# Key exponentials under the activations' second half, w_phi by four loads, layer norm by tiles, and a new order of all steps

## Chip, core and metric

The kernel runs on one core of one Trainium2 chip. The time is device microseconds (us) of one execution, the median of several runs. Engines: TensorE (PE, matmuls; its weight loads are listed as PEld), VectorE (DVE), ScalarE (ACT), GpSimd (POOL) and SyncE (SP, which here only issues DMAs). ACT can issue DMAs too.

## What is computed

One input x (2048 tokens of 448) goes through a layer norm without weights; two branches read the result, and both are added to x.

```python
xn = _layernorm(x)                                   # over 448, eps 1e-5
# A: linear attention, H = 16 heads of Dh = 28
q, k, v = xn @ wqkv
pq, pk = q @ w_phi, k @ w_phi                        # per head, 28 x 28
phi = concat(softmax(p), softmax(-p))                # for q and for k
kv, z = phi_k^T v, sum(phi_k)
o = (phi_q kv) / (phi_q z + 1e-6)
A = o @ wo
# B: feed forward, F = 1792
h = xn @ w1 + b1
B = (h * tanh(softplus(h))) @ w2                     # mish
out = x + A + B
```

The inputs and the output are bfloat16.

## The kernel before, in words

**Units.** The 2048 tokens are 16 tiles t of 128, or 8 units u of two tiles (2u, 2u+1). A unit's normalised pair `xn` is 896 columns; transposed, it is seven blocks of 128 rows, the middle one shared: rows 0 to 63 belong to one tile and rows 64 to 127 to the other. So the matmuls over xn use half the rows of PE at a time (64 rows), two halves side by side into two PSUM banks. `passes` (L418) splits such a block into three parts: A and B (six matmuls each) and H (two, the shared block). A block takes a pair of banks (`pair_part`, L436, `take2`, L390) with its first part and frees it when the last part's reader on ACT or DVE has been recorded. There are four pairs.

**Steps.** `ORDER` (L147) is a hand-kept list of step names; each step appends its instructions to the queues of its engines (`run_order`, L166), so the list is the program order of every engine at once. `Program.resolve` (L89) puts in the semaphore waits. An engine runs its own instructions strictly in that order, the DMAs that SP or ACT issue among them. The names:

- `lx..`, `lkm`, `lkt`, `lvm`, `lqT`, `lp`, `lb`, `l1m`, `l1t`, `l2`, `lo`: loads of x, W_k (main rows and the tails of W_k and W_v), W_v, W_q transposed, w_phi, b1, W1, W2, Wo; the last letter is the issuing queue (s for SP, a for ACT).
- `pi`, `pm`, `pw`, `pv`, `pk`, `pp`, `zero`: constants that POOL sets up. `z12` is twelve matmuls on zeros (`warm`, L369).
- `st`, `rs`, `xn`: layer norm of a unit: mean and variance (`ln_stats`, L459; DVE's bn instructions, or with b the odd tile on ACT), 1/sqrt (`ln_rstd`, L477; a on ACT, p on POOL), and the scaled pair (`ln_pair`, L491; d on DVE, p on POOL). `xt`: the pair's transpose (`xT`, L524), by PE with copies on ACT or DVE, or by a DMA of SP (m).
- `wtk`, `wmk`, `wmq`, `bd`: q and k are never formed: W_q and W_k are multiplied by w_phi first (`w_tr` L555, `w_mm` L578), w_phi lying block-diagonally in `Wbd`, which `w_bd` (L547) fills from `Wraw` and a mask.
- `v`, `k`, `q` with unit and part: the products of xn with W_v and the two folded weights. `k` and `q` end with two exponentials on ACT (plus and minus), into `E_of(u)` (L230) and `Eq_of(u)` (L235).
- `kn`u.s: one half's sums over the 28 features on DVE, their reciprocals, and the product on POOL (`k_norm`, L633). `kv`: 16 matmuls a unit, all units into one pair of banks; `kvz`: DVE takes it out, a DMA transposes it.
- `e`t: a DMA transpose of a tile's query exponentials (L695). `nd`t: 16 short matmuls for numerators and denominators, then seven DVE instructions (L723). `ot`u: transpose of the attention's result. `wo`: its product with Wo.
- `f`q.c: one block of 128 of the 1792 hidden features for half q of the tokens (q = 0 or 1, 1024 tokens), then one mish on ACT into `actT` (`ffn1`, L706). `g`t: 14 full-row matmuls with W2 for a tile (`ffn2`, L831). The last of a tile's `wo` and `g` adds x on DVE (`finish`, L798), and `sto`, `stt` store.

**Shared memory.** `actT` holds for each of 14 feature blocks a row of 2048 tokens. The key exponentials of unit u lie in row 6 + u of it, columns 0 to 1791, so they cover a part of both halves; query exponentials use rows 4 and 5 and a buffer of their own in turn. A mish over such a row waits for all that read it.

**Rows.** Blocks in parts and `nd` use half-row matmuls; the transposes, the weight products, `kv` and `g` use more than 64 rows. PE changes from one row mode to the other 14 times after the warm-up.

Of the kernel before, what the change touches and what calls it, by code (L numbers as in the profile page):

```python
# [170 lines left out]
def _kernel(es, nc, A_x, A_wqkv, A_w_phi, A_wo, B_w1, B_b1, B_w2, out):  # L171
# [284 lines left out]

    def ln_stats(u, both=False):  # L459
# [527 lines left out]
```

## Time and profile before

| | us |
|---|---|
| time, median of 3 runs | 155.51 (154.67, 155.51, 155.71) |
| span of the profiled execution, first to last instruction | 153.4 |
| busy: PE, PEld, DVE, ACT, POOL | 145.5, 74.4, 105.3, 73.3, 40.1 |

The page gives the span of the profiled execution and no run time for it. Times in rows are microseconds from the start of this span. A timeline row is: start, length, engine, source line, operation, what is written and read, count, and in brackets the idle time before it and what ended it; neighbouring instructions of a kind are merged. A row of a window is its bounds, its length, and the busy time of PE, PEld, DVE, ACT and POOL with their counts, the granted clock of PE, the busy share of the DMA engines and what they moved. A row of DMA issues gives count, size and the median time from issue to landing.

### The profile page before, as it was taken

Reading aid. Unit: us, or ns where it says so; the run is one execution under the profiler, and the core shown is the slowest. Engines: PE = TensorE matmul, PEld = TensorE weight load, DVE = VectorE, ACT = ScalarE, POOL = GpSimd, SP = SyncE. Lnnn points to the kernel's source line nnn. Section 1 sums busy time; section 2 is a strip of 40 time slices with the busy share of each in tenths; the row PEclk is TensorE's granted clock in tenths of the full one; section 3 lists DMA queues with packets and bytes.
Section 4 is the critical chain, followed back from the end, with each engine's and each line's share of the span. In section 5 each row is a group of like instructions: output and inputs, shape, how many; then the busy total and the mean of one; then the engine's idle time right before and its main releaser. Section 6 shows DMA issues by size and latency. Waiting matters only on the chain.

```text
span 153.4 us, 3609 instructions
## 1 busy us (share of the span) xinstructions
PE 145.5 (95%) x1541; PEld 74.4 (48%) x1541; DVE 105.3 (69%) x229; ACT 73.3 (48%) x89; POOL 40.1 (26%) x58
## 2 busy tenths in 40 slices
PE   6898998999899999999988999999999999999993
PEld 2364553554344475445434446554555555545552
DVE  1699999999999903078767399995699600693521
ACT  4974998684899896967674673000500000000000
POOL 5562384465999991000000000000000000000000
PEclk9999999999999999999999999999999999999999
DMA  4996656797989309898990303303020320005331
GB/s 128 251 272 198 145 88 133 184 300 148 131 140 195 77 0 85 172 268 164 338 139 14 60 4 64 60 0 60 27 99 0 75 44 4 0 0 129 122 113 60
DMA packets 39964, 17.22 MB, mean 112 GB/s; under 512 B 33932, under 2 KB 39180, under 8 KB 39948
## 3 DMA queue, kind: packets, MB, share of 16 engines
q1 hardware_dynamic: 39776, 16.89, 52.0%
q8 instruction: 12, 0.20, 0.5%
q10 hardware_dynamic: 172, 0.10, 0.2%
q14 instruction: 4, 0.03, 0.1%
...
## 4 chain that ended last, share of the span: by engine, by line
PE 71%; DVE 17%; DMA 6%; POOL 2%; issue 1%; ACT 1%; DVEq 0%; POOLq 0%
PE PS L433 29%; PE PS L836 28%; PE PS L853 7%; DVE xn L507 5%; DMA Wkv<-xn 4%; PE PS L374 3%; DVE stats L472 3%; PE PS L657 2%; PE PS L731 2%; DMA xnT<-xn 2%; DVE Sk L636 2%; DVE v_all L522 2%; POOL xn L502 1%; ACT actT L689 1%; DVE mv L474 1%
## 5 line engine op out<-in xcount | busy, mean ns | idle before, releaser
L433 PE MATMUL PS<-xnT,W 64*128 64x512 bf16 x392 | 45.3, 376 | 0.4 <-DVE v_all L752 0.4
L708 ACT ACTIVATE actT<-PS,b1T 128x1024 bf16<-128x1024 f32 x28 | 30.2, 1113 | 27.2 <-PE PS L433 27.2
L836 PE MATMUL PS<-W,actT 128*128 128x448 bf16 (+1 forms) x224 | 42.7, 351 | 0.0
L836 PEld LDWEIGHTS PS<-W,actT 128*128 128x128 bf16 x224 | 21.6, 98 | 20.2 <-issue 0.7
L433 PEld LDWEIGHTS PS<-xnT,W 64*128 64x128 bf16 x392 | 17.8, 94 | 22.5 <-PE PS L433 2.4
L640 POOL TENSOR_TENSOR actT<-actT,rSk 128x896 bf16<-128x896 bf16 x16 | 26.7, 1699 | 4.8 <-DVE rSk L638 4.8
L801 DVE TENSOR_TENSOR x_all<-PS,x_all 128x448 bf16<-128x448 f32 (+1 forms) x16 | 9.4, 616 | 18.9 <-PE PS L836 15.5
L636 DVE TENSOR_REDUCE Sk<-actT 128x32 f32<-128x896 bf16 x16 | 16.7, 1046 | 0.0
L433 PE MATMUL PS<-Wpk,xnT 64*128 64x448 bf16 x112 | 13.8, 349 | 1.1 <-DMA xnT<-xn 0.7
L628 ACT ACTIVATE actT<-PS 128x896 bf16<-128x896 f32 x16 | 13.7, 927 | 2.4 <-PE PS L433 2.4
L433 PE MATMUL PS<-Wkv,xnT 64*128 64x448 bf16 x112 | 13.6, 349 | 0.0
L433 PE MATMUL PS<-Wpq,xnT 64*128 64x448 bf16 x112 | 12.7, 349 | 0.4 <-ACT actT L689 0.4
L746 DVE COPY Sq<-PS 128x16 f32<-128x16 f32 x32 | 4.0, 167 | 12.5 <-PE PS L731 12.5
L757 DVE TENSOR_TENSOR xn<-v_all,rden 128x448 bf16<-128x448 f32 x16 | 10.0, 625 | 2.4 <-DMA Wkv<-xn 1.9
L472 DVE BATCH_NORM_STATS2 stats<-x_all 128x6 f32<-128x448 bf16 x14 | 8.4, 601 | 3.4 <-DMA x_all<-in_A_x_dram 3.4
L754 DVE TENSOR_TENSOR v_all<-v_all 128x464 f32<-128x464 f32 x16 | 10.3, 642 | 0.6
L750 DVE TENSOR_TENSOR v_all<-PS,Sq 128x464 f32<-128x464 f32 x16 | 10.3, 641 | 0.5
L752 DVE TENSOR_TENSOR v_all<-PS,Sq 128x464 f32<-128x464 f32 x16 | 10.1, 630 | 0.0
L689 ACT ACTIVATE actT<-PS 128x896 bf16<-128x896 f32 x10 | 8.6, 917 | 3.0 <-PE PS L433 2.9
L507 DVE TENSOR_SCALAR xn<-x_all,mv,rstd 128x448 bf16<-128x448 bf16 (+2 forms) x21 | 9.5, 507 | 0.1
L433 PEld LDWEIGHTS PS<-Wpk,xnT 64*128 64x128 bf16 x112 | 5.3, 94 | 6.7 <-DVE v_all L522 1.6
L433 PEld LDWEIGHTS PS<-Wpq,xnT 64*128 64x128 bf16 x112 | 5.4, 94 | 6.1 <-ACT actT L689 0.8
...
## 6 DMA issues: line engine op xcount, KB each, us to landing
...
out_dram<-x_all SPq DMA_DIRECT2D x7, 224.0 KB, 2.1
...
x_all<-in_A_x_dram SPq DMA_DIRECT2D x4, 224.0 KB, 3.2
...
W<-in_B_w_dram SPq DMA_DIRECT2D x2, 224.0 KB, 3.6
```

What stands on the lines that cost most here:

```text
L433: ins = e.matmul(o, lhs(c, k), rhs(c, k), start=first and n == at[par][0], stop=last and n == at[par][-1])
L472: op("DVE", lambda e, t=t: e.bn_stats(stats[:, t, :], x_all[:, t, :]), r=[("x", t)], w=[("st", t)], tag=f"bn{t}")
L507: op("DVE", lambda e, t=t, lo=lo, hi=hi, at=at: e.tensor_scalar(X[:, at:at + hi - lo], x_all[:, t, lo:hi], mv[:, t, 0:1], rstd[:, t:t + 1] ...
L628: op("ACT", lambda e, s=s: e.activation(E_of(u)[:, s, :, :], two(b, D), ACT.Exp, scale=1.0 if s == 0 else -1.0), r=[pb(b), pb(b + 1)], w=[ ...
L636: op("DVE", lambda e: e.tensor_reduce(Sk[u][:, s, :], Eh(), AX.X, ALU.add), r=[("E", u, s)], w=[("Sk", u, s)], tag=f"Sk{u}.{s}")
L640: op("POOL", lambda e: e.tensor_tensor(Eh(), Eh(), ap_on(rSk[u][:, s, 0:1], [[1, 2 * H], [0, DH]]), ALU.mult), r=[("E", u, s), ("rSk", u, ...
L689: op("ACT", lambda e, s=s: e.activation(Eq_of(u)[:, :, s, :].rearrange("p i (h n) -> p i h n", n=64)[:, :, :, 0:QP], two(b, D).rearrange(" ...
L708: op("ACT", lambda e: e.activation(actT[:, fc, q * 1024:(q + 1) * 1024], bank(b, 2), ACT.Mish, bias=b1T[:, fc:fc + 1]), r=[("b1T",), pb(b) ...
L750: op("DVE", lambda e: e.tensor_tensor(tv(t1[i]), num(0), sx(1), ALU.mult), r=[pb(b), pb(b + 1), ("Sq", i, 1)], w=[("t1", i)], tag=f"ta{t}")
L754: op("DVE", lambda e: e.tensor_tensor(t1[i], t1[i], t2, ALU.add), r=[("t1", i), ("t2",)], w=[("t1", i)], tag=f"tc{t}")
L836: ins = e.matmul(bank(b)[:, 0:width(t)], actT[:, fc, tok(t)], W2[:, fc, 0:width(t)], start=first and fc == 0, stop=last and fc == FC - 1)
L853: ins = e.matmul(bank(b)[:, 0:w], oT_of(u)[lo:hi, cc * P:(cc + 1) * P], Wo[lo:hi, cc, 0:w], start=first and n == at[par][0], stop=last and ...
```

## The change

- **Where exponentials lie.** `actT` is laid out by halves of the tokens. All eight key blocks lie in the second half (q = 1) one after another; query exponentials of units 1, 4, 7 and 2, 5 lie in the first half's rows 10, 11 and 12, 13. A mish of the second half now waits for the key blocks under it (`E_under`), one of the first half for none of them.
- **w_phi.** Four small DMAs put its blocks straight into `Wbd`, after `pw` has cleared it. `Wraw`, the mask (`pm`) and the two products on POOL (`bd`) go.
- **Layer norm by tiles.** `st`t, `xn`t (and `rt`t for the root of one tile, `rs`u for two) are steps of one tile each, on DVE (d), ACT (a) or POOL (p). In the new order ACT takes the statistics of tile 5 and scales tile 0; POOL scales tiles 4, 5, 8, 11, 12 and 13; DVE does the rest. Before, ACT took the statistics of tiles 5 and 7, POOL scaled tiles 10 and 11.
- **Loads of x** by any run of tiles. The first part of the loads is divided: ACT issues tiles 1, 4 and 5, 2 and 3, w_phi, W_v, 6 and 7, later 12 to 15, and Wo; SP tiles 0, W_k, the tails, 8 and 9, b1, W_q transposed, later 10 and 11.
- **`kc`u** (`k_norm2`): sums and reciprocals of both halves of a key block in one instruction each; used for units 2 and 3.
- **All steps in a new order.** kv now stands behind f0.0, f0.2, f0.3, f0.4, f0.5 and f0.8, with q6 and a part of q3 behind it. PE changes the row mode 12 times after the warm-up.

The diff, cut to its core:

```diff
 ORDER = """
-table lx2s pw lba zero pv pm st2b lx3s lkms lps st3b lkts z12 pi rs2p rs3a lx1s b1 xn2d wtk0b lvms lx4s xn3d xt2b
-wtk1b bd wmk0b st1 xt3a v2Ad st5 wmk1a pk lqT2 v3Ha lqT0 rs1a lqT1 v2Ha v3Aa lqT3 pp v2Bd qd xn1d k2H v3Ba lx0s k2A
-rs5p wmq0d wmq1a k2B k3A k3H q2B st4 rs4p k3B lx6s xt1m xn5p q3A q2A q2H st7 k1B rs7p st6 l1ts q3B xt5m xn4d rs6p xn7d
-kn3.0 q1B q3H k1A xt4m xt7m v1Bd k1H q1A v1Ad xn6d k5B v1Hd q1H k5A k5H st0 v5Hd rs0p v5Ad kn1.0 xt6m k4B v5Bd k7A
-l1ms kn5.0 k4A v7Hd k4H k7H v7Aa k7B v6Ad xn0d v7Ba k6H kn5.1 v6Ha k6A v6Bd e3 kn2.0 kn7.1 xt0m q4B k6B e2 v4Bd q4A
-q4H kn1.1 v4Hd v4Ad k0A kn6.0 kn3.1 v0Ba k0B e7 v0Aa e6 k0H v0Ha q6H q6A f1.2B q6B f0.0H f1.2A f0.2B kn2.1 f1.2H e4
-f0.2A kn4.0 f0.2H f1.3A e5 f0.0B f1.3H kn6.1 kn4.1 kn7.0 f0.0A f0.1B f1.3B q5A f0.1A e13 f0.1H e8 q7B q5H e9 ep f0.12A
-q7H q0B e12 q7A f0.12B q0A kn0.1 q5B kn0.0 q0H e11 kv5 kv2 kv3 kv6 kv7 kv4 kv1 kv0 kvz f1.1A f1.1H f1.6B f1.1B e0
-f1.6A f0.12H f0.9B los e10 f1.11H f1.6H e15 e14 f0.9A f0.13B f0.9H l2s f0.13A f0.13H f1.13A nd0 f1.11B f1.13H f1.11A
-f0.6A f1.13B f0.6B nd3 f1.7A f0.6H f1.7H f0.4B f1.7B nd2 f0.4H f0.4A e1 f0.7B f0.5H f0.7H ot1m f0.7A f1.10A f0.5A
-f1.4B nd7 f0.5B f1.10B f1.4H f1.10H f1.4A f0.3B nd1 f0.3H f0.11H f0.11A f1.8H f0.3A f1.5A f0.11B f1.5B f1.8B ot0m
-f1.5H f0.10B nd5 f1.8A f0.10H f0.10A f0.8B f1.9B nd4 f0.8A f0.8H f1.9H f1.9A wo1B ot2m nd6 wo1H ot3m nd13 wo1A nd12 g2
-g0 g3 g1 nd11 ot6m f1.12B f1.0A f1.12H f1.0B wo0H wo0A f1.0H wo0B wo2A wo2H sto0 f1.12A wo6H nd9 sto1 wo6A wo2B wo6B
-nd10 nd8 ot4m g5 g12 ot5m g4 g11 g9 g10 g13 wo4H nd14 wo4B wo3A wo5H wo3H wo5A nd15 ot7m wo3B g6 sto6 g7 g8 sto3 wob
-wo5B wo7B wo4A wo7A sto2 wo7H sto5 g14 sto4 g15 stt14 stt15
+pi lx1.2a pw table lx0.1s lx4.6a lx2.4a zero st1d lpa st5a st0d st4d st2d rs0p lvma rs2p lx6.8a xn0a xn1d lkms xn5p
+lkts xn4p lx8.10s lbs st3d z12 wtk0a rt2a wtk1d xt0b lqT3 rt3a wmk0d wmk1a pp b1 xt2b xn2d st8d lqT1 lqT2 lqT0 xn3d
+st9d k0B lx12.14a k2B xt1m st7d qd lx10.12s lx14.16a rt8p pv st6d k0A k0H st12d rt9p k2H v2Ba v0Ba v2Ha v2Aa v0Aa rs3p
+st13d xn6d l1ts st15d xn7d xt3m v0Ha wmq1a wmq0a k2A rt12p rt13p xn13p xn12p st10d xt6m xn8p st14d k1A v1Bd k1B st11d
+q2B k1H rs5p v1Ad q1H q2H v1Hd rt14a q1B xn10d q2A xn9d xn14d rt15p pk xt4m q0A q1A q0B k3B xn15d xt7m v6Ba k3H q0H
+v6Aa xn11p kn0.1 k6H v6Ha k3A kn0.0 xt5m kn1.1 l1ms k6A v3Ad kc3 k6B v3Hd k7A v3Bd k7H v4Hd kn6.0 e3 v4Ad k7B v4Bd k4B
+v7Ba k4H k4A e2 k5B kn7.1 v7Aa kn7.0 q4H k5A v7Ha kc2 e0 k5H q4A e5 f0.0B q4B f0.0H v5Bd f0.0A e9 f0.8H f0.8A v5Ad
+kn5.0 f0.3B f0.8B v5Hd f0.3A e1 f0.4B f0.3H e8 q3B f0.4A f0.5A f0.4H f0.5H f0.2H f0.2A kn1.0 f0.5B kn4.1 q5H e4 q5A
+f0.2B q3H kn6.1 loa q7B q5B q7A q7H kn5.1 kn4.0 kv2 kv6 ep kv1 kv0 kv5 kv7 kv4 kv3 q3A f1.0B kvz f0.9A e10 f1.0A f1.0H
+e14 f0.9H e15 f0.6A f0.9B f0.7B f0.6H nd0 f0.7A f0.6B f0.11H f0.11A f0.7H f0.10B nd3 f0.11B f0.12A f0.10A e11 e6
+f0.10H nd1 f0.12H e7 ot0m f0.1B f0.12B f0.1A f0.1H q6A q6H f1.13H nd2 q6B f1.5A f1.13A f1.4A f1.13B f1.5H f1.1H f1.1A
+f1.4B f1.1B f1.5B f1.6A f1.6H e12 f1.4H ot1m f1.11A f1.6B f1.11B nd4 f1.12H f1.11H l2s f1.12A f0.13B f1.12B f1.7A nd5
+f1.7H f0.13H f0.13A f1.2H f1.7B ot2m f1.2A nd7 wo0H f1.2B wo1B wo0A wo1A nd6 ot3m wo1H wo0B nd10 g2 g7 g3 g1 g0 nd12
+e13 f1.10A f1.10H f1.9A f1.9H wo3B f1.10B nd13 f1.9B wo3A wo3H f1.8B ot6m f1.3H nd11 f1.3A ot5m g6 g5 f1.8H nd15 f1.8A
+wo2H f1.3B sto1 wo2B nd14 nd9 wo2A nd8 g4 sto3 g14 g9 sto2 g12 ot7m g8 ot4m g13 wo7H wo4B wo7A wo5A wo6A wo5H wo6H
+wo4A wob wo5B wo4H wo6B wo7B sto0 g10 g11 g15 sto6 stt14 sto5 sto4 stt15
 """
...
-    actT = sb("actT", [P, FC, S], BF16)
+    actT = sb("actT", [P, 2, FC, S // 2], BF16)
...
-    FE = FC - NU
+    def act_flat(q):
+        return actT[:, q, :, :].rearrange("p f n -> p (f n)")
 
     def E_of(u):
-        return actT[:, FE + u, 0:4 * D].rearrange("p (s i d) -> p s i d", s=2, i=2)
-
-    EQ_ROWS = (None, 4, 5)
+        return act_flat(1)[:, u * 4 * D:(u + 1) * 4 * D].rearrange("p (s i d) -> p s i d", s=2, i=2)
+
+    def E_under(fc):
+        return range(fc * 1024 // (4 * D), ((fc + 1) * 1024 - 1) // (4 * D) + 1)
+
+    EQ_ROWS = (None, 10, 12)
 
     def Eq_of(u):
-        if u % 3 == 0:
-            return Eq0[:, :].rearrange("p (i s c) -> p i s c", i=2, s=2)
-        return actT[:, EQ_ROWS[u % 3], :].rearrange("p (i s c) -> p i s c", i=2, s=2)
+        src = Eq0[:, :] if u % 3 == 0 else act_flat(0)[:, EQ_ROWS[u % 3] * 1024:(EQ_ROWS[u % 3] + 2) * 1024]
+        return src.rearrange("p (i s c) -> p i s c", i=2, s=2)
 
...
     def load_phi(eng):
-        dma(eng, lambda e: e.dma_start(Wraw[:], A_w_phi.rearrange("(g j) d f -> (j d) g f", j=4)), w=[("Wraw",)],
-            tag="ldWphi")
+        src = A_w_phi.rearrange("(g j) d f -> j d g f", j=4)
+        for j in range(4):
+            r, c = divmod(j, 2)
+            dma(eng, lambda e, j=j, r=r, c=c: e.dma_start(Wbd[j * DH:(j + 1) * DH, :, r, c * DH:(c + 1) * DH], src[j]),
+                r=[("Wbd0",)], w=[("Wbd", j)], tag="ldWphi")
...
-    def ln_stats(u, both=False):
...
-    def ln_rstd(u, eng):
...
-    def ln_pair(u, eng):
...
+    def ln_stats(t, eng):
...
+    def ln_rstd(a, n, eng):
...
+    def ln_tile(t, eng):
+        X, i = xn[(t // 2) % NXN], (t // 2) % NXN
+        if eng != "DVE":
+            op("DVE", lambda e: e.scalar_tensor_tensor(shift[:, t:t + 1], mv[:, t, 0:1], -1.0, rstd[:, t:t + 1], ALU.mult,
+                                                       ALU.mult), r=[("mean", t), ("rstd", t)], w=[("sh", t)], tag=f"sh{t}")
+        for n, (lo, hi, at) in enumerate([(0, D, 0)] if t % 2 == 0 else [(384, D, D), (0, 384, D + 64)]):
+            src, dst = x_all[:, t, lo:hi], X[:, at:at + hi - lo]
+            r, w = [("x", t), ("mean", t), ("rstd", t)], [("xn", i, t % 2, n)]
+            if eng == "DVE":
+                op("DVE", lambda e, src=src, dst=dst: e.tensor_scalar(dst, src, mv[:, t, 0:1], rstd[:, t:t + 1],
+                                                                      op0=ALU.subtract, op1=ALU.mult), r=r, w=w, tag=f"xn{t}.{n}")
+            elif eng == "ACT":
+                op("ACT", lambda e, src=src, dst=dst: e.activation(dst, src, ACT.Identity, bias=shift[:, t:t + 1],
+                                                                   scale=rstd[:, t:t + 1]), r=r + [("sh", t)], w=w, tag=f"xn{t}.{n}")
+            else:
+                op("POOL", lambda e, src=src, dst=dst: e.tensor_scalar(dst, src, rstd[:, t:t + 1], shift[:, t:t + 1],
+                                                                       op0=ALU.mult, op1=ALU.add), r=r + [("sh", t)], w=w, tag=f"xn{t}.{n}")
...
-    def w_bd():
-        for r in range(2):
...
+    def k_norm2(u):
+        def Eh(s):
+            return E_of(u)[:, s, :, :].rearrange("p i (h f) -> p (i h) f", f=DH)
+        op("DVE", lambda e: e.tensor_reduce(Sk[u][:, :, :].rearrange("p s n -> p (s n)"),
+                                            E_of(u).rearrange("p s i (h f) -> p (s i h) f", f=DH), AX.X, ALU.add),
+           r=[("E", u, 0), ("E", u, 1)], w=[("Sk", u, 0), ("Sk", u, 1)], tag=f"Sk{u}")
+        op("DVE", lambda e: e.reciprocal(rSk[u][:, :, :], Sk[u][:, :, :]), r=[("Sk", u, 0), ("Sk", u, 1)],
+           w=[("rSk", u, 0), ("rSk", u, 1)], tag=f"rSk{u}")
+        for s in range(2):
+            op("POOL", lambda e, s=s: e.tensor_tensor(Eh(s), Eh(s), ap_on(rSk[u][:, s, 0:1], [[1, 2 * H], [0, DH]]), ALU.mult),
+               r=[("E", u, s), ("rSk", u, s)], w=[("E", u, s)], tag=f"phik{u}.{s}")
...
-            op("ACT", lambda e: e.activation(actT[:, fc, q * 1024:(q + 1) * 1024], bank(b, 2), ACT.Mish,
-                                             bias=b1T[:, fc:fc + 1]),
-               r=[("b1T",), pb(b), pb(b + 1)],
-               w=[("act", fc, q)] + ([("E", fc - FE, s) for s in range(2)] if fc >= FE else
-                                     [x for i in range(3) if EQ_ROWS[i] == fc for x in (("Eq", i, 0), ("Eq", i, 1), ("Eqp", i))]), tag=f"mish{q}_{fc}")
+            under = [("E", u, s) for u in E_under(fc) for s in range(2)] if q else [
+                x for i in (1, 2) if EQ_ROWS[i] == fc - fc % 2 for x in (("Eq", i, 0), ("Eq", i, 1), ("Eqp", i))]
+            op("ACT", lambda e: e.activation(actT[:, q, fc, :], bank(b, 2), ACT.Mish, bias=b1T[:, fc:fc + 1]),
+               r=[("b1T",), pb(b), pb(b + 1)], w=[("act", fc, q)] + under, tag=f"mish{q}_{fc}")
...
-    def tok(t):
+    def act_of(fc, t):
         u, par = t // 2, t % 2
-        col = (u // 4) * 1024 + par * 512 + (u % 4) * P
-        return slice(col, col + P)
+        col = par * 512 + (u % 4) * P
+        return actT[:, u // 4, fc, col:col + P]
```

More of the change, by code (lines that the diff above doesn't have):

```diff
@@ L178, in _kernel @@
     ident = sb("ident", [P, P], BF16)
-    mask = sb("mask", [GP, 4], FP32)
-    Wraw = sb("Wraw", [GP, G, DH], BF16)
     Wbd = sb("Wbd", [GP, G, 2, 64], BF16)
@@ L479, in ln_rstd @@
+    def ln_rstd(a, n, eng):
+        b = a + n
+        r, w = [("mv", t) for t in range(a, b)], [("rstd", t) for t in range(a, b)]
         if eng == "POOL":
             op("POOL", lambda e: e.tensor_scalar(lnv[:, a:b], mv[:, a:b, 1], float(LN_EPS), 0.0, op0=ALU.add,
-                                                 op1=ALU.add),
-               r=[("mv", a), ("mv", a + 1)], w=[("lnv", u)], tag=f"vare{u}")
-            op("POOL", lambda e: e.tensor_tensor(rstd[:, a:b], lnv[:, a:b], mhalf[:], ALU.pow),
-               r=[("lnv", u), ("eps",)], w=[("rstd", u)], tag=f"rstd{u}")
+                                                 op1=ALU.add), r=r, w=[("lnv", t) for t in range(a, b)], tag=f"vare{a}")
+            op("POOL", lambda e: e.tensor_tensor(rstd[:, a:b], lnv[:, a:b], mhalf[:, 0:n], ALU.pow),
+               r=[("lnv", t) for t in range(a, b)] + [("eps",)], w=w, tag=f"rstd{a}")
@@ new lines, in ln_rstd @@
+           r=[("lnv", t) for t in range(a, b)], w=w, tag=f"rstd{a}")
+    def ln_tile(t, eng):
[15 more added lines that the diff above has]
+                                                                       op0=ALU.mult, op1=ALU.add), r=r + [("sh", t)], w=w, tag=f"xn{t}.{n}")
@@ L543, in xT @@
              [("xnT", u), ("xnU", u)], f"xTe{u}")
-    def w_bd():
-        for r in range(2):
-            op("POOL", lambda e, r=r: e.tensor_tensor(
-                Wbd[:, :, r, 0:QP].rearrange("p g (j f) -> p g j f", f=DH),
-                ap_on(Wraw[:, 0, 0:1], [[DH, G], [0, 2], [1, DH]]),
-                ap_on(mask[:, 2 * r:2 * r + 1], [[0, G], [1, 2], [0, DH]]), ALU.mult),
-               r=[("Wraw",), ("mask",), ("Wbd0",)], w=[("Wbd", r)], tag=f"Wbd{r}")
     def w_tr(h, eng):
@@ L592, in mm @@
             return ins
-        pe(mm, ([("WT", h), ("WU", h)] if which else [("WqT", g) for g in range(G)] + [("WqTd",)]) + [("Wbd", 0), ("Wbd", 1)], [pb(b), pb(b + 1)], f"wmm{which}{h}")
+        pe(mm, ([("WT", h), ("WU", h)] if which else [("WqT", g) for g in range(G)] + [("WqTd",)]) + [("Wbd", j) for j in range(4)], [pb(b), pb(b + 1)], f"wmm{which}{h}")
         if which and eng == "both":
@@ L817, in f @@
             for fc in range(FC):
-                ins = e.matmul(to, actT[:, fc, tok(t)], W2[:, fc, CUT:D], start=False, stop=fc == FC - 1)
+                ins = e.matmul(to, act_of(fc, t), W2[:, fc, CUT:D], start=False, stop=fc == FC - 1)
             return ins
@@ L835, in f @@
             for fc in range(FC):
-                ins = e.matmul(bank(b)[:, 0:width(t)], actT[:, fc, tok(t)], W2[:, fc, 0:width(t)],
+                ins = e.matmul(bank(b)[:, 0:width(t)], act_of(fc, t), W2[:, fc, 0:width(t)],
                                start=first and fc == 0, stop=last and fc == FC - 1)
@@ L875, in _kernel @@
     for u in range(NU):
-        add(f"st{u}", ln_stats, u)
-        add(f"st{u}b", ln_stats, u, True)
         add(f"xt{u}b", xT, u, "both")
+        add(f"kc{u}", k_norm2, u)
         for eng, c in (("ACT", "a"), ("POOL", "p")):
-            add(f"rs{u}{c}", ln_rstd, u, eng)
-        for eng, c in (("DVE", "d"), ("POOL", "p")):
-            add(f"xn{u}{c}", ln_pair, u, eng)
+            add(f"rs{u}{c}", ln_rstd, 2 * u, 2, eng)
         for eng, c in (("ACT", "a"), ("DVE", "d"), ("DMA", "m")):
@@ L901, in _kernel @@
         add(f"stt{t}", store, t, t + 1)
+        for eng, c in (("ACT", "a"), ("DVE", "d"), ("POOL", "p")):
+            add(f"st{t}{c}", ln_stats, t, eng)
+            add(f"rt{t}{c}", ln_rstd, t, 1, eng)
+            add(f"xn{t}{c}", ln_tile, t, eng)
     for h in range(2):
@@ L929, in _kernel @@
     add("qd", double_qT)
-    for n, fn in (("pi", p_ident), ("pm", p_mask), ("pw", p_wbd), ("pv", p_ones), ("pk", p_mask2), ("pp", p_pads), ("zero", p_zero)):
+    for n, fn in (("pi", p_ident), ("pw", p_wbd), ("pv", p_ones), ("pk", p_mask2), ("pp", p_pads), ("zero", p_zero)):
         add(n, fn)
-    for n in (1, 2, 4, 8, 12):
+    for n in range(1, 17):
         add(f"z{n}", warm, n)
```

67 lines of the change are left out of this document (17 added, 50 removed).

## The prediction

> **What bounds the kernel now.** First the page:
>
> ```profile
> span 153.4 us, 3609 instructions
> PE 145.5 (95%) x1541; PEld 74.4 (48%) x1541; DVE 105.3 (69%) x229; ACT 73.3 (48%) x89; POOL 40.1 (26%) x58
> ```
>
> TensorE (PE) works nearly all the time, and the new order issues the same 1541 matmuls. Only the start, the holes and the tail can move. To find holes I take PE's pace from start-to-start distances in its timeline.
>
> ```profile
> 14.41 0.96 PE L590 MATMUL PS<-Wbd,WqT 112*128 112x112 bf16 x16 [0.45 <-DVE WqT L287]
> 15.30 1.50 PE L433 MATMUL PS<-Wpk,xnT 64*128 64x448 bf16 x14
> ...
> 17.77 1.49 PE L433 MATMUL PS<-Wpq,xnT 64*128 64x448 bf16 x14
> 19.10 0.73 PE L433 MATMUL PS<-Wpk,xnT 64*128 64x448 bf16 x6
> ```
>
> ```profile
> 58.45 7.32 PE L433 MATMUL PS<-xnT,W 64*128 64x512 bf16 x66
> 65.61 0.39 PE L731 MATMUL PS<-KVZ,EqT 56*128 56x60 bf16 x16
> ...
> 76.91 3.21 PE L433 MATMUL PS<-xnT,W 64*128 64x512 bf16 x28
> 80.78 0.40 PE L731 MATMUL PS<-KVZ,EqT 56*128 56x60 bf16 x16 [0.66 <-DMA EqT<-Eq]
> 81.00 2.12 PE L433 MATMUL PS<-xnT,W 64*128 64x512 bf16 x18
> 83.50 3.63 PE L433 MATMUL PS<-xnT,W 64*128 64x512 bf16 x32 [0.39 <-DVE v_all L752]
> ...
> 94.05 10.77 PE L836 MATMUL PS<-W,actT 128*128 128x448 bf16 x56
> 104.75 0.39 PE L731 MATMUL PS<-KVZ,EqT 56*128 56x60 bf16 x16
> ...
> 112.79 18.71 PE L836 MATMUL PS<-W,actT 128*128 128x448 bf16 x98
> 131.43 0.36 PE L853 MATMUL PS<-Wo,WqT 64*128 64x448 bf16 x2
> ```
>
> A block of q, k, v or output (14 half-row matmuls) takes 19.10 - 17.77 = 1.33, so a part of six 0.57 and a part of two 0.19. A W1 block takes 14/66 of 65.61 - 58.45, 1.52. Seven output tiles take 18.64 and four 10.70: 2.65 each, and 0.1 is left for each change out of the full-row mode. By this pace 28 matmuls from 76.91 should end at 79.95, and 18 from 81.00 at 82.95. PE lost 0.83 and 0.55 there, **1.4 us**. SyncE's timeline tells why: the transpose issued right behind the W2 load held the queue 5.31 us, so e1, and the freeing of DVE's work behind it, came late.
>
> ```profile
> 69.89 0.59 SPq L301 DMA_DIRECT2D W<-in_B_w_dram  x1
> 70.53 5.31 SPq L697 DMA_TRANSPOSE EqT<-Eq  x1
> ```
>
> Then the early stage, by windows (length; busy time of PE, PEld, DVE, ACT, POOL), and by the timelines of VectorE (DVE) and GpSimd (POOL):
>
> ```profile
> 2.30:3.15 0.85, 0.85 (x4) 0.30 (x3) 0.00 (x0) 0.00 (x0) 0.64 (x5) 1.00 0.99 347
> 3.38:5.08 1.70, 1.70 (x5) 0.61 (x4) 1.50 (x4) 1.63 (x6) 0.00 (x0) 1.00 0.83 207
> 30.00:40.00 10.00, 9.63 (x102) 4.87 (x98) 9.86 (x14) 6.99 (x9) 6.98 (x5) 1.00 1.15 224
> ```
>
> ```profile
> 8.21 0.91 DVE L507 TENSOR_SCALAR xn<-x_all,mv,rstd 128x448 bf16<-128x448 bf16 x3
> ...
> 22.35 1.08 DVE L636 TENSOR_REDUCE Sk<-actT 128x32 f32<-128x896 bf16 x1
> 23.47 0.35 DVE L638 RECIPROCAL rSk<-Sk 128x32 f32<-128x32 f32 x1
> 23.74 2.18 DVE L507 TENSOR_SCALAR xn<-x_all,mv,rstd 128x448 bf16<-128x448 bf16 x3
> ```
>
> ```profile
> 23.90 1.70 POOL L640 TENSOR_TENSOR actT<-actT,rSk 128x896 bf16<-128x896 bf16 x1 [1.39 <-DVE rSk L638]
> ...
> 37.95 19.93 POOL L640 TENSOR_TENSOR actT<-actT,rSk 128x896 bf16<-128x896 bf16 x12 [0.62 <-DVE rSk L638]
> ```
>
> DVE is busy 9.86 of 10 us there. The three xn instructions of a pair take 0.91 alone and 2.18 beside a key product of POOL. At the end POOL multiplies twelve key halves without a break, 1.66 each, until 57.88; kv needs them all, and the first W1 matmul behind kv starts at 58.45. So before 58 PE, DVE and POOL are about equally tight, and after it PE alone counts.
>
> **The change part by part.** Times are in the span of the profiled execution, 153.4. The page gives no run time for that execution; the median of the three runs, 155.51, is 2.1 above the span, and I keep this offset.
>
> *Front.*
>
> ```profile
> 1.42 4.75 PE L374 MATMUL PS<-zeros 128*128 128x512 bf16 x12 [1.42 <-POOL zeros L317]
> ```
>
> ```profile
> x_all<-in_A_x_dram SPq DMA_DIRECT2D x4, 224.0 KB, 3.2
> ...
> Wraw<-in_A_w_phi_dram SPq DMA_DIRECT2D x1, 24.5 KB, 4.4
> ```
>
> pi (the 0.85 us from 2.30) now precedes pw and zeros, so the warm-up ends at 7.0 instead of 6.2; W_k's transposes then run to 7.9. Tiles 4 and 5 stand second on ACT's queue: issued near 1.3, landed near 4.5 by the 3.2. ACT's statistics of tile 5 take 1.7 (the window from 3.38): to 6.3. The phi loads on ACT's queue must wait for pw, near 2.2, and behind them wait these statistics, the W_v load and x tiles 6 and 7; tile 5 comes later than that anyway, and W_v, issued near 6, is wanted at 13.3. xn0 on ACT, then the first W_k copy (7.6 to 8.7, estimated at 1.1 for 1024 columns), the square roots of pairs 2 and 3, half of xT0 and the second key product's copy follow one another on ACT: about 0.5 + 0.5 + 0.5 + 0.9, to 11.1. DVE's copies end at the same time. So the first key block starts near **11.2**. The last phi load, issued near 3.7, lands near 8.1 by the 4.4; its product comes at 8.75, so it is covered with 0.6 to spare. The masks and the two mask products that go were beside other work: nothing.
> Before, PE had at 15.30 also done v2, v3 and eight matmuls of k2, (28 + 8)/14 x 1.33 = 3.4, and the q-weight products, 0.9. Without them it would stand at 11.0. The two fronts are equal within 0.2.
>
> *From 11 to 57.* POOL gets six of sixteen layer-norm tiles instead of two and ACT one, and every xn lies ahead of the key products, so none is blocked. I walked the new order through the four pairs of PSUM banks. From 13.3 on ACT does exponentials (0.87 each, below), v copies and now both q-weight copies almost without a gap. PE waits for a bank from ACT several times, 0.1 to 0.3 each, 1.0 in all. Once it waits about 1.0 for DVE: v7 takes the pair of v3, whose copy stands on DVE behind kc3, a sum of both halves (twice 1.08) that itself waits for k3's second exponential near 30.7. Without waits kv would start at 11.2 + 40.0 (22.6 blocks of 1.33, six of 1.52, the q products) = 51.2; with them at **53.2**. POOL's products start at 26.3, pause 2.3 (mostly for kc3) and end at 26.3 + 16 x 1.66 + 2.3 = 55.2. The seventh kv step wants the last one at 55.5: just covered. kv ends at 56.5, 1.95 before 58.45. But q6 and six matmuls of q3 are left over, 1.9, against 2/14 of a W1 block and more done ahead, 0.2. Gain: 1.95 - 1.7 = **0.25**. That key exponentials lie under the second halves allows any first half before kv; the order has six blocks there against five and twelve of 14 matmuls, so the freedom itself is worth nothing yet.
>
> *From 57 on.* l2s now stands behind e12 and ot1, near 77.4. No transpose follows until ot2, which waits for nd5 near 87; before, the queue was clear at 80.78, 11 us after the load's issue, so at worst 88.5. First use of W2 is at 91. The **1.4** is saved. It costs 0.25 that ACT issues four Wo loads ahead of q5's exponentials, and 0.3 that f1.4 waits for nd2's banks. Net **0.85**. q6 comes late, with two more table loads, but ACT is ahead by then. Mode changes fall from 14 to 12, all of it in the front and already in its sum; the tail is unchanged.
>
> ```profile
> 42.97 1.73 ACT L689 ACTIVATE Eq<-PS 128x896 bf16<-128x896 f32 x2
> 44.71 1.28 ACT L708 ACT_TABLE_LOAD   x1
> 46.00 1.11 ACT L708 ACTIVATE actT<-PS,b1T 128x1024 bf16<-128x1024 f32 x1
> ```
>
> A table load takes 1.28, with no gap to its neighbours. [...]
>
> Sum: -0.25 - 0.85 = -1.1: **154.4 us**. Unknown: the front, -0.5 (copies that overlap) to +1.5 (loads of two queues delaying each other); the waits in the middle, 0.5 to 3.5 instead of 2.0.
>
> **Rivals.**
> *A, forecast*: 154.4, chance 0.48, own range 153.3 to 155.5.
> *B, the key chain comes earlier.* POOL starts near 25 and has no pause, so the products end near 52; PE has no wait over 0.3. kv ends 1.9 earlier: 152.5. For it: DVE loses the blocked xn, 1.27 each. Against: kc3's wait is in the order. 0.19.
> *C, it only reshuffles.* POOL's xn4 and xn5 (7.5 to 9.3) hold DVE as a product held it (2.18 against 0.91); the copies of W_k's second half and of xT0 slip, and the front by 1.1: 155.5. Against: those read PSUM, and no row shows such a copy held. 0.18. [...]
> *D, slower: the four phi loads.* Third on ACT's queue, they compete with x tiles and with the q-weight transposes that SP issues from 4.0. When the last lands after 8.75, every later step, ACT's and POOL's chains too, moves one for one. It decides from a landing at 11.4; at 12 the time is 157.7. For it: 24.5 KB took 4.4 before. Against: those 4.4 were spent mostly behind W_k. 0.15.
>
> **How the numbers follow.** 1% is 1.56 us, about what a measurement of this kernel tells from no change: faster means below 153.95, slower above 157.07. Faster is all of B and 0.38 of A: 0.37. Slower is most of D (0.12) and 0.02 of the others: 0.14. The rest is 0.49. The range runs from B's end to where D begins: 152.4 to 157.0.
>
> **What would show it.** Right: the first Wpk matmuls near 11.2; kv from 53 to 56.5; a hole of about 1 us near 34, ended by a DVE copy to v_all; no hole behind the W2 load. Wrong: a first key block after 12.5, POOL's products ending after 57, or new PE waits of over 1 us in all behind 57.

## The result, and the profile after

The changed kernel takes **153.96 us** (median of 153.23, 153.96 and 154.09) against 155.51: ratio 0.989, interval 0.984 to 0.994. A second measurement gave 153.78 against 155.22, 0.991 (0.988 to 0.993). The forecast, 154.4, was 0.4 too high: the sign was right, 1.1 of the 1.55 us were foreseen, and the steps differ. The page, to be held against the one of before:

```profile
span 152.2 us, 3611 instructions
PE 144.6 (95%) x1541; PEld 76.1 (50%) x1541; DVE 101.1 (66%) x223; ACT 75.7 (50%) x90; POOL 44.3 (29%) x65
```

The span is 1.2 shorter, as the median is 1.6. Where it came from, by PE's time beyond its pace (start to start, as in the prediction; the point of equal work is the 11.0 that the prediction works out from 15.30):

| stretch | before | after | change |
|---|---|---|---|
| to the first key block (before: the point of equal work) | | | +0.8 |
| from there to the first block behind kv | 2.8 | 2.3 | -0.5 |
| from there to the last W2 tile | 2.2 | 0.7 | -1.6 |

The last W2 tile starts at 146.79 instead of 148.03, 1.24 earlier; the first row is what is left of that. It is good to some 0.3 only: in the eight profiled kernels that have this front, the changed one and its repetition among them, the first key block starts between 11.61 and 12.26.

**Front.** PE's, ACT's, DVE's and GpSimd's timelines, one after another:

```profile
8.99 0.56 PE L504 MATMUL PS<-ident,xn 128*128 128x128 bf16 x7 [0.65 <-ACT xn L495]
9.90 0.96 PE L571 MATMUL PS<-Wbd,Eq 112*128 112x112 bf16 x16 [0.34 <-ACT Eq L509]
...
11.92 1.31 PE L429 MATMUL PS<-Wpk,xnT 64*128 64x448 bf16 x12 [0.45 <-ACT Wpk L509]
```

```profile
8.17 0.76 ACT L495 ACTIVATE xn<-x_all,shift,rstd 128x448 bf16<-128x448 bf16 x1 [1.06 <-DVE shift L486]
8.84 1.00 ACT L509 ACTIVATE Eq<-PS 112x1024 bf16<-112x1024 bf16 x1
```

```profile
7.25 0.63 DVE L466 BATCH_NORM_STATS2 stats<-x_all 128x6 f32<-128x448 bf16 x1 [0.99 <-DMA x_all<-in_A_x_dram]
...
8.01 0.12 DVE L486 SCALAR_TENSOR_TENSOR shift<-mv,rstd 128x1 f32<-128x1 f32 x1
...
9.44 0.66 DVE L511 COPY Eq<-PS 112x1024 bf16<-112x1024 bf16 x1
```

```profile
8.81 1.75 POOL L498 TENSOR_SCALAR xn<-x_all,rstd,shift 128x64 bf16<-128x64 bf16 x3 [0.59 <-DVE shift L486]
```

Read backwards: the first key block waits for ACT's W_k copies, which stand behind xn0; xn0 waits for a one-column shift on DVE, and that shift stands behind st2, which waited 0.99 us for tiles 2 and 3 to land. DVE's copy from PSUM at 9.44 ran its 0.66 us inside GpSimd's 1.75: it did not wait for GpSimd to end.

**Middle.** Two PE waits are left between 11.92 and 57.10 where before, from 15.30 to 58.45, had five of 0.2 to 0.6 us (2.4 together). The timelines of PE, DVE and GpSimd:

```profile
34.21 0.74 PE L429 MATMUL PS<-Wkv,xnT 64*128 64x448 bf16 x6 [0.59 <-DVE v_all L511]
...
52.87 3.24 PE L650 MATMUL PS<-actT,v_all 128*60 128x112 bf16 x124
56.88 0.29 PE L650 MATMUL PS<-actT,v_all 128*60 128x112 bf16 x4 [0.78 <-issue]
57.10 0.74 PE L429 MATMUL PS<-Wpq,xnT 64*128 64x448 bf16 x6
```

```profile
30.60 2.02 DVE L627 TENSOR_REDUCE Sk<-actT 128x64 f32<-128x1792 bf16 x1 [1.72 <-ACT actT L609]
32.65 0.55 DVE L630 RECIPROCAL rSk<-Sk 128x64 f32<-128x64 f32 x1
33.12 1.03 DVE L511 CAST v_all<-PS 128x896 bf16<-128x896 f32 x1
```

```profile
45.03 9.99 POOL L621 TENSOR_TENSOR actT<-actT,rSk 128x896 bf16<-128x896 bf16 x6
```

The first wait was forecast; start to start it costs 0.77. The second was not: four matmuls from the end of kv PE stood still for 1.0 us from start to start, and "issue" says that it waited for nothing that the profile shows.

**Late.** From 57.10 on PE has no wait at all, only seven changes of row mode of 0.1. The W2 load and the transpose behind it on SyncE, and PE there:

```profile
77.59 1.18 SPq L306 DMA_DIRECT2D W<-in_B_w_dram  x1
87.64 1.23 SPq L757 DMA_TRANSPOSE Wkv<-xn  x1
```

```profile
72.20 8.79 PE L429 MATMUL PS<-xnT,W 64*128 64x512 bf16 x80
80.84 0.38 PE L723 MATMUL PS<-KVZ,EqT 56*128 56x60 bf16 x16
81.06 3.18 PE L429 MATMUL PS<-xnT,W 64*128 64x512 bf16 x28
```

The transpose behind the load comes 10 us later, and no PE wait follows it.

### The profile page after: what moved, and what is told of

Same layout as the page of the kernel before. It is cut to its first block, busy times and chain, and to the rows that moved or that the text cites. A ratio compares the mean times of both kernels' runs of the same rounds, so it can differ in the third digit from the quotient of the medians.

```text
span 152.2 us, 3611 instructions
## 1 busy us (share of the span) xinstructions
PE 144.6 (95%) x1541; PEld 76.1 (50%) x1541; DVE 101.1 (66%) x223; ACT 75.7 (50%) x90; POOL 44.3 (29%) x65
## 4 chain that ended last, share of the span: by engine, by line
PE 78%; ACT 12%; DMA 4%; DVE 3%; issue 1%; ACTq 0%
PE PS L429 38%; PE PS L828 28%; PE PS L845 7%; DMA x_all<-in_A_x_dram 4%; ACT actT L609 3%; PE PS L723 2%; PE PS L650 2%; ACT actT L682 2%; ACT v_all L509 2%; DVE Sk L627 1%; ACT Wpq L509 1%; ACT Eq L682 1%; DVE v_all L511 1%; ACT Eq L509 1%; ACT Wpk L509 1%
## 5 line engine op out<-in xcount | busy, mean ns | idle before, releaser
L429 PE MATMUL PS<-xnT,W 64*128 64x512 bf16 x392 | 46.2, 376 | 0.0
L621 POOL TENSOR_TENSOR actT<-actT,rSk 128x896 bf16<-128x896 bf16 x12 | 20.0, 1699 | 0.0
L429 PE MATMUL PS<-Wpk,xnT 64*128 64x448 bf16 x112 | 13.3, 349 | 0.5 <-ACT Wpk L509 0.5
L466 DVE BATCH_NORM_STATS2 stats<-x_all 128x6 f32<-128x448 bf16 x15 | 9.2, 614 | 5.2 <-DMA x_all<-in_A_x_dram 5.2
L617 DVE TENSOR_REDUCE Sk<-actT 128x32 f32<-128x896 bf16 x12 | 12.5, 1043 | 0.0
L429 PEld LDWEIGHTS PS<-Wkv,xnT 64*128 64x128 bf16 x112 | 5.4, 94 | 6.0 <-DVE v_all L511 1.0
```

The costliest lines, as they stand in the source:

```text
L429: ins = e.matmul(o, lhs(c, k), rhs(c, k), start=first and n == at[par][0], stop=last and n == at[par][-1])
L617: op("DVE", lambda e: e.tensor_reduce(Sk[u][:, s, :], Eh(), AX.X, ALU.add), r=[("E", u, s)], w=[("Sk", u, s)], tag=f"Sk{u}.{s}")
L621: op("POOL", lambda e: e.tensor_tensor(Eh(), Eh(), ap_on(rSk[u][:, s, 0:1], [[1, 2 * H], [0, DH]]), ALU.mult), r=[("E", u, s), ("rSk", u, ...
```

## The experiments

Theory: the W2 load's place gives most of the late gain; the middle is shorter by its order alone, not by the layout or the shared layer norm; what it could still give is eaten by the front and by the stall in kv. The times are medians, each with its own runs of before; the ratio is to those. The medians of before lie between 154.87 and 155.51, so kernels that were not measured beside each other are better compared by their ratios, or by stretches of their profiles. Fragments of ORDER stand for the order. A hole is a stretch in which PE stands still.

### The W2 load alone, in the kernel before

```diff
-... e15 e14 f0.9A f0.13B f0.9H l2s f0.13A ... f0.5H f0.7H ot1m f0.7A
+... e15 e14 f0.9A f0.13B f0.9H f0.13A ... f0.5H f0.7H ot1m l2s f0.7A
```

> The kernel before with one step moved: the W2 load stands right behind the freeing of ot1 instead of right ahead of it, so that no transpose is queued behind it for some 10 us. My theory: PE's two holes at e1 (0.83 and 0.55 us in the profile of before) close, and the time falls by 1.3 us, 0.9 to 1.5. Rival (the late gain of the change comes from the other order of the feed-forward steps or from the activations' new layout, and the holes before come from DVE being late anyway): two holes of over 0.3 us remain ahead of the steps that take e1's output, and the time stays within 0.4 us of before.

154.36 against 155.22, ratio 0.994 (0.992 to 0.996): **-0.9 us**. PE there:

```profile
79.92 0.39 PE L731 MATMUL PS<-KVZ,EqT 56*128 56x60 bf16 x16
80.15 2.12 PE L433 MATMUL PS<-xnT,W 64*128 64x512 bf16 x18
82.50 1.69 PE L433 MATMUL PS<-xnT,W 64*128 64x512 bf16 x14 [0.23 <-DVE v_all L752]
```

The hole of 0.83 is gone; of the one of 0.55, 0.39 (start to start) stayed. DVE, which ends it, still waits 0.91 us (before 1.88) for the transpose of ot1, and this was issued at 75.84, as before at 75.88: the hold of the queue had not delayed it. That is the low end of my theory, with a part of the rival. So one step out of the whole order gives 0.9 of the late 1.6 us. The rest came with the new order of the feed-forward blocks, under which that hole doesn't show; no run tests it alone.

### The changed kernel again, and the stall in kv

> The changed kernel once more, as the yardstick of this call and to see whether the hole of 0.8 us inside the last kv step comes back (no wait stands there). If it belongs to the order of the program and its instruction supply: again a hole of 0.6 to 1.1 us, between the last eight matmuls of kv. If it was an accident of one execution: none over 0.2. The time: 153.9 us, 1.2 to 1.9 below before.

153.78; the hole is there again, larger:

```profile
56.86 0.29 PE L650 MATMUL PS<-actT,v_all 128*60 128x112 bf16 x4 [1.05 <-issue]
```

It is no accident. One DMA queue, q8, carries twelve blocks of 16 KB of instructions, by their number those of PE (see the last section). With the Wo loads moved to SyncE:

```diff
-... q3H kn6.1 loa q7B ... e10 f1.0A f1.0H e14 f0.9H e15 f0.6A
+... q3H kn6.1 q7B ... e10 f1.0A f1.0H e14 f0.9H e15 los f0.6A
```

> The changed kernel with the four Wo loads issued by SyncE behind e15 (as before) and no longer by ACT ahead of q5's exponentials, near 51 us. Theory 1: the hole in the last kv step is late instruction supply, a block of instructions whose transfer is held up by the Wo loads; then the hole is gone, and with the 0.25 us of ACT's issuing the time falls by 0.8 to 1.3 us. Theory 2: the hole comes from the place in the program alone, whatever else is moving; then the hole stays at 0.8 us and the time falls by 0 to 0.3. Theory 3: SyncE's loads now stand ahead of transposes that are wanted, as the W2 load did before; then new PE holes of 0.5 to 1.4 us show between 60 and 75 us, and the time does not fall.

154.49, ratio 0.996 (0.993 to 0.998): 0.7 slower than the changed kernel beside it, but theories 1 and 3 are both right. PE, ACT and SyncE:

```profile
52.60 3.34 PE L650 MATMUL PS<-actT,v_all 128*60 128x112 bf16 x128
...
71.40 0.39 PE L723 MATMUL PS<-KVZ,EqT 56*128 56x60 bf16 x16 [1.06 <-ACT actT L703]
```

```profile
70.23 2.12 ACT L703 ACTIVATE actT<-PS,b1T 128x1024 bf16<-128x1024 f32 x2 [2.30 <-DMA EqT<-actT]
```

```profile
62.76 2.32 SPq L313 DMA_DIRECT2D Wo<-in_A_wo_dram  x4
65.12 1.31 SPq L690 DMA_TRANSPOSE EqT<-actT  x1
```

kv runs its 128 matmuls through. But the loads now stand ahead of e11, e6 and e7. The transpose e11, issued at 65.12, landed 5.0 us later; it holds the mish of f0.12, which writes over its source, until 70.23, and the mish holds PE. Then the loads at an idle hour of SyncE:

```diff
-... q5H e4 q5A f0.2B q3H kn6.1 loa q7B
+... q5H e4 los q5A f0.2B q3H kn6.1 q7B
```

> The changed kernel with the four Wo loads issued by SyncE behind e4's transpose, near 47 us, where SyncE has nothing to do until 57, and no longer by ACT at 50.6. Theory: the hole in the last kv step comes from instructions that arrive late. In the runs so far the 16 KB block of instructions that is fetched around kv began 0.1 us before kv with no loads under way (no hole), 1.1 us after kv's start (hole of 0.35) and 1.6 to 1.7 after it (holes of 0.8 and 1.05) with the Wo loads under way. With the loads over by 52.5 the block comes at kv's start and the hole is gone; ACT's queue is also free of 2.1 us of issuing; no other hole appears. The time falls by 1.0 to 1.4 us against the changed kernel, to about 152.6. Rival: moved loads only move the trouble, as they did when SyncE issued them at 62.8 (a new hole of 1.06 at q6): then the loads hold the transposes of the key side or the V copies near 47 to 52, kv starts 0.5 to 1 us later, and the time stays within 0.3.

152.90, ratio 0.987 (0.984 to 0.990): **0.9 to 1.1 us under the changed kernel** by the medians, 0.4 to 0.6 by the ratios; kv in one piece, no new wait. The profiles agree: from the first key block to kv's end PE takes 44.2 us instead of 45.2, and from there to the last W2 tile 89.7 in both. The cause is seen in the DMA view, where q10 carries the Wo loads and q8 the instructions. First the changed kernel from 52.8 to 54.4, then from 54.4 to 54.6; last the kernel with the early loads and the split sum (the last one below), from 52.2 to 52.6, where kv starts at 52.45:

```profile
DMA packets 690, 0.59 MB, mean 371 GB/s; under 512 B 28, under 2 KB 690, under 8 KB 690
...
q10 hardware_dynamic: 690, 0.59, 109.6%
```

```profile
q10 hardware_dynamic: 70, 0.05, 90.3%
q8 instruction: 1, 0.02, 34.8%
```

```profile
DMA packets 1, 0.02 MB, mean 41 GB/s; under 512 B 0, under 2 KB 0, under 8 KB 0
...
q8 instruction: 1, 0.02, 18.0%
```

With Wo in the queues the instruction block starts 1.6 us after kv; without, it starts 0.2 before. Over all versions of the changed kernel the hole goes with that lag:

| instruction block starts, after kv | hole in kv |
|---|---|
| 1.74 (again), 1.71 (old layout), 1.56 (the changed kernel), 1.52 (phi late) | 1.24, 0.97, 0.97, 0.97 |
| 1.26 (layer norm on DVE), 1.07 (split), 0.95 (front) | 0.83, 0.54, 0.51 |
| 0 or earlier (the five versions that load Wo elsewhere) | none |

The hole always stands behind kv's 124th matmul, and in all seven cases PE goes on 2.3 to 2.6 us after the block's start. Without a hole the 125th matmul comes 3.05 us after kv's start, so by this estimate a block that is over 0.4 to 0.7 us late costs time.

### The wait for v3's copy

```diff
-... v3Ad kc3 k6B v3Hd k7A v3Bd k7H
+... v3Ad kn3.0 k6B v3Hd k7A v3Bd kn3.1 k7H
```

> The changed kernel with the key sum of block 3 in two halves: the first where it was, the second behind the copy of v3's last heads, so that the copy no longer waits for k3's second exponential. Theory: the hole of 0.77 us at 34 (v7 waits for DVE's copy of v3) closes, all behind it comes 0.6 to 0.8 earlier as far as kv, and GpSimd's products, which start block 3 earlier by half, do not hold kv; the time falls by 0.5 to 0.8 us. Rival: PE is only set free to wait for the next bank or at kv for GpSimd's products (their chain ends at 55.0 and is DVE's and GpSimd's own time); then another hole of 0.5 us or more shows between 34 and 57 and the time stays within 0.2.

153.07 beside 153.78 for the changed kernel, ratio 0.985 (0.983 to 0.987): **-0.7**, and the hole at 34 is gone. PE there:

```profile
33.10 0.73 PE L429 MATMUL PS<-Wkv,xnT 64*128 64x448 bf16 x6
33.67 1.49 PE L429 MATMUL PS<-Wpk,xnT 64*128 64x448 bf16 x14
```

From the first key block to kv's start PE takes 40.2 us, 0.7 less than in the changed kernel. The span fell by 1.3: kv's hole happened to be 0.4 smaller as well, and the first key block came 0.3 earlier. The forecast wait was real and on the path.

### The front

```diff
-st0d st4d st2d rs0p ... xn1d lkms ... lbs st3d z12 ... lqT3 rt3a wmk0d wmk1a pp b1 xt2b xn2d
+st0d st4d rs0p ... xn1d st2d lkms ... lbs z12 ... lqT3 wmk0d st3d wmk1a pp b1 xt2b rt3a xn2d
```

> The changed kernel with the statistics of tile 2 behind xn1 on DVE, those of tile 3 behind the first mask-free copy of W_k, and pair 3's square root behind xT2's first half, so that the shift of tile 0, xn0 on ACT and the W_k copies behind it no longer wait for tile 2 to land (6.9 to 7.2 us). Theory: that wait made the first key block 0.4 to 0.7 later than I forecast; it now starts near 10.9 instead of 11.6 to 11.9, all behind it moves with it, and the time falls by 0.5 to 0.8. Rival: the front is held by another link at the same time (the landing of W_k's second rows, near 7.7, or GpSimd's xn4 and xn5), then the first key block moves by less than 0.3 and the time stays within 0.3; or the pair 1 norms come late and PE gets a hole of the same size near 14 to 17.

153.70, ratio 0.992 (0.989 to 0.995): no gain that can be told from the changed kernel, so the rival was nearer than my theory. The first key block came at 11.33, 0.3 ahead of the earliest of the eight with the changed kernel's front, and behind its first part PE ran into a hole of 0.44. PE, in best2, which has the same front:

```profile
9.52 0.95 PE L571 MATMUL PS<-Wbd,Eq 112*128 112x112 bf16 x16 [0.61 <-DMA Wbd<-in_A_w_phi_dram]
...
11.47 0.74 PE L429 MATMUL PS<-Wpk,xnT 64*128 64x448 bf16 x6 [0.40 <-ACT Wpk L509]
12.48 1.69 PE L429 MATMUL PS<-Wpk,xnT 64*128 64x448 bf16 x16 [0.27 <-DVE xnT L511]
```

With the statistics out of the way the four phi loads end the wait, near 9.5, not at the 8.1 that I forecast. In the changed kernel the product waited until 9.90 for ACT's copy, so, if they landed as in best2, the loads were covered by 0.4 at most. On top of best2 I then issued them one load earlier (and put the statistics of tile 3 behind xT2's copy):

```diff
-pi lx1.2a pw table lx0.1s lx4.6a lx2.4a zero st1d lpa
+pw pi lx1.2a zero table lx0.1s lx4.6a lpa lx2.4a st1d
```

> The three edits of best2, with the front taken further: on GpSimd the cleared phi block before the identity and the zeros before it, so that ACT can issue the four phi loads one load earlier (ahead of tiles 2 and 3), and the statistics of tile 3 behind xT2's copy on DVE. In best2 the product of W_k with phi waited 0.6 us for the last phi load (issued 3.81, landed near 9.5), and the first key block ran into a second hole of 0.45 us behind those statistics. Theory: the phi loads were hidden by 0.1 to 0.4 us in the changed kernel and became the gate when the rest of the front went earlier; issued 0.5 earlier they land near 9.0, the first key block starts near 11.1 and the second hole goes: 0.5 to 0.8 us earlier at 12.4. But GpSimd's key products ended at 54.4 in best2 while the last kv step began at 54.96: about 0.5 us of that can be used; the time falls by 0.2 to 0.5 against best2, to about 151.8. Rival: the landing of W_k's second rows (near 7.75) or GpSimd's xn4 and xn5 hold the front, or tile 2's later landing opens a hole near 13 to 16; then the time stays within 0.2 of best2.

153.64, ratio 0.992 (0.989 to 0.995): 1.4 worse than best2, and the expectation fell. The profiled execution, the shortest of the eight at 152.99, shows 0.6 of it, in the first key block, at 12.06 instead of 11.47; the rest stays open. Tiles 2 and 3 now land last, and DVE's statistics of tile 2 hold the W_k copy behind them:

```profile
8.70 0.63 DVE L466 BATCH_NORM_STATS2 stats<-x_all 128x6 f32<-128x448 bf16 x1 [1.68 <-DMA x_all<-in_A_x_dram]
...
9.57 0.69 DVE L511 COPY Eq<-PS 112x1024 bf16<-112x1024 bf16 x1
```

In the three orders tried, each makes another load the last: the front seems held by the sum of what is loaded before 9 us, but no run loads less. To price a late front I moved the phi loads far back:

```diff
-... zero st1d lpa st5a st0d
+... zero st1d st5a lpa st0d
```

> The changed kernel with the four phi loads issued by ACT behind the statistics of tile 5, near 6.3 to 8.2 us instead of 2.3 to 4.2 (the W_v load and tiles 6 and 7 go 1.9 later with them). It prices the rival of four small loads. In best2 the last phi load, issued at 3.8, held the product of W_k with phi until 9.5: 5.7 from issue to use. Theory: issued at 7.8 it lands near 12.5 to 13.5, the product starts 3 to 3.8 us later than the 9.6 to 9.9 of the changed kernel, the first key block near 15, and the time rises by 2.5 to 3.8 us, nearly one for one, because every chain of the middle hangs on that block. Rival: the middle has room (the layer norms of DVE and GpSimd run ahead in the meantime and take the later waits away), so that less than half of the delay, under 1.7 us, reaches the end.

156.72 over all twelve executions; the ratio of 1.006 (1.002 to 1.010) leaves out the five longest. The edit did something else than meant. ACT's and PE's timelines:

```profile
10.06 0.76 ACT L495 ACTIVATE xn<-x_all,shift,rstd 128x448 bf16<-128x448 bf16 x1 [2.78 <-DVE mv L467]
```

```profile
10.87 0.56 PE L504 MATMUL PS<-ident,xn 128*128 128x128 bf16 x7 [2.32 <-ACT xn L495]
11.78 1.03 PE L571 MATMUL PS<-Wbd,Eq 112*128 112x112 bf16 x16 [0.34 <-ACT Eq L509]
...
13.82 3.29 PE L429 MATMUL PS<-Wpk,xnT 64*128 64x448 bf16 x22
```

ACT's xn0 stands behind those issues on its queue and held PE (the row names DVE, which had long been done). The phi loads, the last issued at 8.0, had landed by 11.78, at most 3.8 us later. The first key block started at 13.82, 1.9 late, not 3 to 3.8 as I expected. Three executions with a granted clock of 1.00 took 154.82, 155.15 and 155.74; their middle is 0.3 above its own before and so 1.7 above the changed kernel: as far as three executions show, the 1.9 us of the front reach the end nearly one for one, as rival D had it. Four at 0.989, the profiled one among them, took 156.40 to 156.86; what they have more goes with PE's clock. Windows of PE (bounds, length, busy, clock, DMA share, GB/s):

```profile
11.00:12.00 1.00, 0.66 (x12) 1.00 1.06 370
12.00:13.00 1.00, 1.00 (x19) 0.77 0.27 100
13.00:14.00 1.00, 0.97 (x9) 0.50 0.00 0
14.00:15.00 1.00, 1.00 (x8) 0.50 0.17 22
15.00:16.00 1.00, 1.00 (x10) 0.53 0.87 272
16.00:17.00 1.00, 1.00 (x14) 1.00 0.43 165
```

### The layout, and the layer norm on GpSimd

The layout of before under the new order (six hidden blocks change their numbers):

```diff
-    actT = sb("actT", [P, 2, FC, S // 2], BF16)
+    actT = sb("actT", [P, FC, S], BF16)
...
-    EQ_ROWS = (None, 10, 12)
+    EQ_ROWS = (None, 4, 5)
```

> The changed kernel's order and all its other edits, with the activations laid out as before (key exponentials under the last eight rows, query exponentials under rows 4 and 5); only the numbers of six hidden rows are exchanged so that the same number of blocks comes ahead of kv. Theory: the layout is worth nothing by itself; the time stays within 0.3 us of the changed kernel. Rival: freedom in the first halves is what lets the middle run without waits, then new holes of 0.5 us or more stand between 36 and 60.

153.75, ratio 0.992 (0.989 to 0.995), the same two holes at 34.3 and 56.9: the layout is worth nothing by itself. Two of the six blocks ahead of kv had to become second halves for it. Four of GpSimd's tiles back on DVE:

```diff
-... rt12p rt13p xn13p xn12p st10d xt6m xn8p ... v6Aa xn11p kn0.1
+... rt12p rt13p xn13d xn12d st10d xt6m xn8d ... v6Aa xn11d kn0.1
```

> The changed kernel with four of GpSimd's layer-norm tiles (8, 11, 12 and 13) given back to DVE, at the same places of the order. Theory: the layer norm by tiles is worth time because DVE is the tighter engine between 15 and 35 us: four tiles of 0.4 us on DVE push its copies and key sums back by 1.0 to 1.6, PE's hole behind v3's copy grows from 0.8 to 1.5 or more or new ones open, and the time rises by 0.5 to 1.5 us. Rival: GpSimd is as tight (its products run to 55.0 and start when the xn tiles are done): DVE has room of that size before 26, and the time stays within 0.3 or falls.

153.74, ratio 0.993 (0.990 to 0.995): no difference; my theory fell, for these four tiles. That the shorter middle is the order's doing is thus argued from what it is not: no run has the new order with all else as before. The hole only changes its place and its name:

```profile
29.42 0.35 PE L429 MATMUL PS<-Wkv,xnT 64*128 64x448 bf16 x2
30.41 0.74 PE L429 MATMUL PS<-Wpk,xnT 64*128 64x448 bf16 x6 [0.65 <-DMA xnT<-xn]
```

A PE that waits at 30.4 for a late transpose doesn't wait at 34 any more.

### Together

Split, early Wo loads and front; then without the front:

> The changed kernel with three edits together: the key sum of block 3 in two halves, the Wo loads on SyncE behind e4, and the front's statistics behind xn1. By the split (0.7), the loads (1.0 to 1.4) and the front (0.5 to 0.8), if they add: 2.2 to 2.9 us under the changed kernel, near 151.2. If GpSimd's products (which end at 54 to 55 whatever PE does) come to hold kv, the last part is lost and it stops near 152.

> The changed kernel with two of best2's three edits: the key sum of block 3 in two halves and the Wo loads on SyncE behind e4; the front as in the changed kernel. Alone the split took 0.7 us off (its profile still had 0.35 to 0.6 of the hole inside kv) and the loads 0.9. Theory: the two add, because the hole behind v3's copy and the hole in kv stand one behind the other on PE: 152.2, and the front edits of best2 (152.21) added nothing that can be measured, since the phi loads held the front there. Rival: they overlap, because GpSimd's products, which end near 54, stop kv as soon as PE arrives earlier: then a wait for GpSimd of 0.4 us or more stands in kv, and the time is 152.7 or more.

152.21, ratio **0.982 (0.979 to 0.985)**, the best version, 2.8 us under before; and 152.33, 0.984 (0.981 to 0.987). The two repairs of the middle add: in the profile of the last kernel PE takes 43.5 us from the first key block to kv's end, 1.7 less than in the changed kernel, and the two holes there were 0.77 and 0.97. Against the repetition of the changed kernel the medians give 1.45 us (of 0.7 and 0.9), the ratios 1.1 (of 0.9 and 0.6). The front's edits add 0.1, which is no difference: best2's first key block comes 0.8 earlier than the last kernel's, but 0.5 of that is lost again before kv's end. GpSimd's products end at 54.74 in the last kernel, kv's last step starts at 55.23, so the rival's wait is half a microsecond away:

```profile
52.45 3.34 PE L650 MATMUL PS<-actT,v_all 128*60 128x112 bf16 x128
```

```profile
44.76 9.98 POOL L621 TENSOR_TENSOR actT<-actT,rSk 128x896 bf16<-128x896 bf16 x6
```

## Why the prediction came out near, point by point

- **Front, forecast equal within 0.2: wrong by 0.7.** The step was "so the first key block starts near 11.2"; it was 11.92 (11.61 to 12.26 over the eight profiles). I followed ACT's queue but not DVE's: the shift that xn0 needs stands behind st2, and st2 waits for tiles 2 and 3 until 7.23. Tiles 4 and 5 also landed at 5.4, not 4.5: their 224 KB took 4.1 us beside other loads, where I used the 3.2 that the page of before gives as the median.
- **Middle, 2.0 us of waits.** The 1.0 behind kc3 was right in place and cause, 0.77 in size, and the split shows that it counted. The other 1.0, ACT's bank waits, didn't appear. kv started at 52.87, 0.3 ahead of the forecast, though PE began 0.7 late.
- **kv's end, forecast 56.5: 57.10.** The stall of 1.0 is the term that I had not at all. I priced the Wo loads on ACT by ACT's time (0.25). ACT did stand 1.1 us for issuing them, but no PE wait came of that; what they cost was the instruction block behind them. So "Gain: 0.25" up to 57 was a loss of about 0.3, by the table above.
- **Late, net 0.85: 1.6.** The two holes went as forecast, 1.4, but not by the cause alone that I gave: moved by itself, the W2 load is worth 0.9, and 0.39 of the second hole stayed in that kernel, behind a transpose that the hold of the queue had not delayed. The two charges, 0.25 and 0.3, never reached PE: it has no wait behind 57.10, so ACT had freed every bank in time. The 0.2 besides is spread over smaller gaps of before.
- **Table load before q5: no wait of PE.** It took 1.28 us, from 53.14, and q5's exponentials followed at 54.44. kv's hole is PE's only one there, and it closes when the Wo loads move while the table load stays.
- **Rivals.** B: the products ended at 55.0, not 52. C: the one copy looked at was not held, and the front was late for another reason. D: the loads landed later than forecast and were just covered; its price of one for one was nearly right, 1.7 of 1.9.

Errors of +0.7 and +1.0 (front, kv) met errors of -1.0, -0.2 and -0.75 (ACT's waits, the size of kc3's, the late stage). Two terms had the right cause, kc3's wait and most of the W2 hole; that the sum was close is luck.
